# A float32 matmul of 256 tokens issued as two of 128, in the first product of a feed-forward

## The chip, the core and the metric

The kernel runs on one NeuronCore of a Trainium2 chip. The metric is the device time of one execution in microseconds; smaller is better. The engines are named as the profile names them: PE (TensorE matmuls), PEld (TensorE weight loads), DVE (VectorE), ACT (ScalarE), POOL (GpSimd) and SP (SyncE, which issues most transfers).

## What is computed

Attention in which a query sees only the keys of its own hash bucket, for 4 x 8 heads of 768 tokens and 64 features; its output, as 3072 tokens of 512 features, goes through a feed-forward with 2048 hidden features and a gate. Everything is float32.

```python
def _attn_ref(q, k, v, proj):
    ...
    mask = q_bucket[:, :, :, None] == k_bucket[:, :, None, :]
    scores = scale * np.matmul(q, k.transpose(0, 1, 3, 2))
    scores = np.where(mask, scores, -1000000000.0)
    ...
    return np.matmul(attn, v).astype(np.float32)

def _moe_ref(x, w_in, w_out):
    h = x @ w_in
    sp = np.maximum(h, 0.0) + np.log1p(np.exp(-np.abs(h)))
    g = h * erf(sp)
    return (g @ w_out).astype(np.float32)
```

The change lies in `h = x @ w_in`, called the first product here; `g @ w_out` is the second.

## The kernel before

Attention comes first, for 16 pairs of heads, and takes until about 312 us of the profiled execution. Its matmuls stand at L387 and L856 (hash bits), L568 (scores `st`, a bfloat16 part and a float32 part, two heads in the two row halves of the array), L653 (`av`, two heads in the two column halves), and L697 (the sums of the softmax). Ten small matmuls at L817 (`warm`) stand ahead of it. The feed-forward follows. An `If` on a flag that the kernel computes chooses between finishing this feed-forward and a slower general way with a feed-forward of its own; the profiled execution runs one feed-forward.

The feed-forward works on 6 tiles of 512 tokens. Each tile has 4 blocks of hidden features, so there are 24 blocks `p`. Both products use Strassen's scheme in Winograd's form: operands are cut into quarters, and 7 products of quarters take the place of 8; for one block a product is [2 x 128 hidden features] x [256 features] x [256 tokens].

The function `product(p, name, where, first, last)` issues one of the seven, P1 to P7. Its result fills a PSUM tile of 128 partitions x 2 x 256 float32 (one bank): partition and `u` are the hidden feature, the last axis is the token. The loop over `u` takes the two halves of the hidden features, that over `kc` the two halves of the 256 features that are summed over. So a product is 4 matmul instructions (L1257), each with 128 x 128 weights `a[:, kc, f : f + P]` (a slice of `w_in_sb` or of sums in `area`) and 256 moving columns `b[:, kc, :]`, the tokens. `start` on the very first clears the bank's accumulation, the later ones add. In the first three blocks (`FILL`) the results go to the banks M1 to M7 and X, later always to the bank X.

After a product either `read` (L1275, ACT copies the bank to `h`) or `complete` (L1279, DVE adds the bank to `h`) empties it. The gate follows on ACT (L1287, L1291, L1308) and DVE (L1297, L1312). `project` (L1375) issues the second product, one instruction at a time, 28 per block, into the banks M1 to M7, which collect over the 4 blocks of a tile.

The order of the work is not written by hand: `arrange` simulates the engines with fixed costs (1.73 for a `product`, 0.432 for a `project`), ranks and dependences, and the operations are emitted in the order it finds. On PE a product alternates with about four instructions of `project` once the pipeline is filled. The program marks its last matmul for the engine that waits for the bank, and its first matmul waits until the bank was emptied.

Of the kernel before, what the change touches and what calls it, by code (L numbers as in the profile page):

```python
# [63 lines left out]
P = 128  # L64
# [133 lines left out]
def kernel(  # L198
# [11 lines left out]
    nc = tc.nc  # L210
# [47 lines left out]
    for ab in range(2):  # L258
        rows = slice(ab * D, ab * D + D)
        nc.vector.tensor_copy(  # L260
            out=proj_sb[rows, ab * QR : ab * QR + NBIT],
# [5 lines left out]
    for c, (end, factor) in enumerate(  # L267
# [12 lines left out]
            out=steps[:, c : c + 1],  # L280
# [9 lines left out]
    for ab in range(2):  # L290
        rows = slice(ab * D, ab * D + D)
        nc.vector.tensor_copy(
            out=proj_q[rows, ab * QB : ab * QB + NBIT],
# [12 lines left out]
    def bank(name):  # L306
        if "X" in kept:
            return kept["X"]
        return misc.tile([P, 512], F32, name=name, tag="bank")
# [907 lines left out]
    def feed_forward(pools, check, late):  # L1217
        again = late is None
        work, outp, sums, hp = (pools[name] for name in ("work", "outp", "sums", "hp"))
        if True:  # L1220
# [8 lines left out]
            def product(p, name, where, first, last):  # L1229

                t, c = divmod(p, NC4)
                d = st[p]
                x = blocks[t % 2]
                b11, t3 = x[:, 0:2, 0:TH], x[:, 0:2, TH:T]
                b21, b22 = x[:, 2:4, 0:TH], x[:, 2:4, TH:T]
                t1, t2, t4 = (x_sum[:, n, :, :] for n in range(3))
                a11, a12 = w_in_sb[:, 0:2, 0:FH], w_in_sb[:, 2:4, 0:FH]
                s3, a22 = w_in_sb[:, 0:2, FH:DFF], w_in_sb[:, 2:4, FH:DFF]
                s1, s2, s4 = (w_sum[:, n, :, :] for n in range(3))
                a, b = dict(  # L1240
                    P1=(a11, b11),
                    P2=(a12, b21),
                    P3=(s4, b22),
                    P4=(a22, t4),
                    P5=(s1, t1),
                    P6=(s2, t2),
                    P7=(s3, t3),
                )[name]
                if first:
                    if where == "X":  # L1250
                        d[where] = bank("X")[:, :].rearrange("p (u t) -> p u t", u=2)
                    else:
                        d[where] = kept[where]
                for u in range(2):
                    f = (2 * c + u) * P
                    for kc in range(2):
                        nc.tensor.matmul(  # L1257
                            out=d[where][:, u, :],
                            lhsT=a[:, kc, f : f + P],
                            rhs=b[:, kc, :],  # L1260
                            start=(first and u == 0 and kc == 0),
                            stop=(last and u == 1 and kc == 1),
                            skip_group_check=True,
                        )

            def quarter(p, q):

# [184 lines left out]
            def first_ops(p):  # L1452
# [25 lines left out]
                for k, (name, where, q, fn) in enumerate(steps):  # L1478
# [5 lines left out]
                    if chain["P"]:  # L1484
# [4 lines left out]
                        1.73,  # L1489
                        (0, p, k),  # L1490
                        product,
                        (p, name, where, name in ("P1", "P2", "P5"), name in ("P4", "P2", "P3")),
                        after=after,
# [217 lines left out]
            for t in range(1, NTILE):  # L1711
                first, last = (t - 1) * NC4, t * NC4 - 1
# [165 lines left out]
```

## Time and profile before

| | us |
|---|---|
| median of 2 runs | 900.13 (900.12 to 900.14) |
| span of the profiled execution | 898.4 |
| attention, until the first matmul of L1257 | 312.5 |
| from the first to the last matmul of L1257 | 312.5 to 854 |
| last matmul of the second product starts | about 894 |

The profiled execution's own time isn't listed apart from its span; the runs' median lies 1.7 us above the span.

In the profile's views a row is a group of instructions: line, engine, operation, tile written <- tiles read, shape, and xcount. In the line's view two numbers follow, busy microseconds and the mean nanoseconds of one; in the timeline a row begins with the start and the length of the group in microseconds from the span's start. A shape of `128*128 128x256` for PE is rows*columns of the array that are used, then the partitions x columns that stream through. PE and PEld are the two halves of TensorE and can be busy at the same time. Matmuls are pipelined: the recorded duration of one is longer than the distance between two.

### The profile page before, as it was taken

The numbers are of one execution on the slowest core, as the hardware profiler recorded it, in microseconds if no ns is written. First come the engines' busy times: TensorE is split into PE (matmuls) and PEld (weight loads), VectorE is DVE, ScalarE is ACT, GpSimd is POOL, SyncE is SP. The second block draws the span as 40 slices with busy tenths as digits, with TensorE's granted clock in tenths as the row PEclk, the third lists the DMA queues.
The fourth block names the chain that finished last, engine by engine and source line by source line (L and its number), as shares of the span: only waits on it lengthen the run. The fifth ranks groups of instructions, "written<-read, shape, count | busy, mean of one in ns | idle before, by whom it ended". The sixth has DMA issues, their size and how long they took to land.

```text
span 898.4 us, 12500 instructions
## 1 busy us (share of the span) xinstructions
PE 893.6 (99%) x4888; PEld 664.0 (74%) x4888; DVE 667.1 (74%) x836; ACT 577.4 (64%) x808; POOL 58.1 (6%) x97
## 2 busy tenths in 40 slices
PE   9999999999999999999999999999999999999998
PEld 5544444444444588888888888888888888888887
DVE  5999999999999879996566556656776556655653
ACT  6888888788887668855555455555655555545520
POOL 1111211111110000000000001000100000000000
PEclk9999999999999999999999999999999999999999
DMA  9557655676651322201231014211321123101321
GB/s 231 132 159 192 188 163 142 182 192 193 165 146 61 102 89 65 82 35 71 59 95 58 25 47 106 82 36 47 99 89 36 36 59 94 35 11 47 97 72 49
DMA packets 65203, 86.95 MB, mean 97 GB/s; under 512 B 34430, under 2 KB 47790, under 8 KB 65136
## 3 DMA queue, kind: packets, MB, share of 16 engines
q1 hardware_dynamic: 56192, 63.55, 25.0%
q0 software_dynamic: 8224, 21.80, 8.6%
q8 instruction: 40, 0.66, 0.3%
q10 hardware_dynamic: 720, 0.72, 0.2%
q14 instruction: 27, 0.22, 0.1%
HBM read 64.71 MB, written 17.40 MB: 91 GB/s over the span
## 4 chain that ended last, share of the span: by engine, by line
PE 99%; DVE 0%; ACT 0%; issue 0%; DVEq 0%
PE M L1375 32%; PE X L1257 29%; PE st L568 17%; PE av L653 14%; PE M L1257 4%; PE bits L856 1%; PE bits L697 1%; PE warm L817 0%; PE X L1375 0%; PE bits L387 0%; PE z_ps L697 0%; DVE u L1412 0%; PE X L697 0%; ACT e_even L595 0%; DVE w L1412 0%; ACT both L400 0%
## 5 line engine op out<-in xcount | busy, mean ns | idle before, releaser
L1297 DVE SCALAR_TENSOR_TENSOR e<-w,e 128x1024 f32<-128x1024 f32 x144 | 173.6, 1220 | 8.4 <-ACT w L1291 3.3
L1257 PE MATMUL X<-area,w_in_sb 128*128 128x256 f32 x680 | 160.6, 379 | 0.0
L1291 ACT ACTIVATE w<-h,cq 128x1024 f32<-128x1024 f32 x144 | 155.5, 1136 | 0.0
L568 PE MATMUL st<-q,k 64*128 64x384 f32 x768 | 155.2, 483 | 0.0
L1279 DVE TENSOR_TENSOR h<-X,h 128x512 f32<-128x512 f32 x65 | 44.7, 688 | 144.8 <-PE X L1257 144.8
L1257 PEld LDWEIGHTS X<-area,w_in_sb 128*128 128x128 f32 x680 | 129.2, 190 | 17.6
L1375 PE MATMUL M<-w_out_sb,h 128*128 128x256 f32 x576 | 141.5, 379 | 0.0
L1257 PE MATMUL X<-area 128*128 128x256 f32 x520 | 122.8, 379 | 0.0
L1275 ACT COPY h<-X 128x512 f32<-128x512 f32 x85 | 49.3, 580 | 112.8 <-PE X L1257 112.6
L1375 PEld LDWEIGHTS M<-w_out_sb,h 128*128 128x128 f32 x576 | 109.4, 190 | 14.9
L1257 PEld LDWEIGHTS X<-area 128*128 128x128 f32 x520 | 98.8, 190 | 13.4
L1287 ACT ACTIVATE e<-h,cq 128x1024 f32<-128x1024 f32 x48 | 55.0, 1148 | 79.3 <-DVE h L1279 79.1
L1375 PE MATMUL M<-wt,S 128*128 128x256 f32 x384 | 95.4, 379 | 0.1
L568 PEld LDWEIGHTS st<-q,k 64*128 64x128 f32 x768 | 69.2, 187 | 35.1 <-issue 33.7
L641 DVE TENSOR_TENSOR area<-area 128x1536 f32<-128x1536 f32 (+1 forms) x46 | 79.2, 1721 | 6.7 <-ACT area L595 5.4
L1375 PEld LDWEIGHTS M<-wt,S 128*128 128x128 f32 x384 | 72.9, 190 | 10.4 <-issue 0.5
L595 ACT ACTIVATE e_even<-st 128x768 f32<-128x768 f32 x96 | 73.9, 818 | 0.5 <-PE st L568 0.5
L595 ACT ACTIVATE area<-st 128x768 f32<-128x768 f32 x90 | 72.7, 810 | 0.3 <-PE st L568 0.3
L653 PE MATMUL av<-e_even,v 128*64 128x385 f32 x384 | 65.7, 490 | 0.0
L568 PE MATMUL st<-both 64*128 64x384 bf16 x384 | 63.9, 324 | 0.2 <-ACT e_even L595 0.2
L1312 DVE TENSOR_TENSOR h<-h,e 128x1024 f32<-128x1024 f32 x48 | 58.0, 1220 | 4.0 <-ACT e L1308 4.0
L653 PE MATMUL av<-area,v 128*64 128x384 f32 x360 | 60.6, 486 | 0.0
(135 smaller groups left out, 965.5 us busy)
## 6 DMA issues: line engine op xcount, KB each, us to landing
wt<-wt SPq DMA_DIRECT2D x24, 768.0 KB, 4.3
raw<-in_w_out_dram POOLq DMA_DIRECT2D x16, 512.0 KB, 4.1
raw<-in_w_in_dram POOLq DMA_DIRECT2D x14, 512.0 KB, 4.4
v<-in_v_dram SPq DMA_DIRECT2D x32, 192.0 KB, 4.8
q<-in_qkT_dram SPq DMA_DIRECT2D x30, 192.0 KB, 3.9
k<-in_qkT_dram SPq DMA_DIRECT2D x30, 192.0 KB, 4.6
r<-rd SPq DMA_DIRECT2D x30, 192.0 KB, 3.8
xs<-x SPq DMA_DIRECT2D x15, 384.0 KB, 3.1
```

Of the source, the lines that this page charges most:

```text
L568: nc.tensor.matmul(out=st[:, ab, 0:HS], lhsT=d["k" + src][rows, keys], rhs=d["q" + src][rows, cols], start=(part == 0), stop=(part == 1),)
L595: nc.scalar.activation(out=e[:, :, 0:HS], in_=st[:, :, 0:HS], func=AF.Exp, scale=scale)
L641: nc.vector.tensor_tensor(out=into, in0=one, in1=two, op=ALU.add)
L653: nc.tensor.matmul(out=d["av", half][rows, 0:w], lhsT=d["v"][:, g * GC + c, rows], rhs=e[:, ab, 0:w], start=(g == 0 and c == 0), stop=(g = ...
L1257: nc.tensor.matmul(out=d[where][:, u, :], lhsT=a[:, kc, f : f + P], rhs=b[:, kc, :], start=(first and u == 0 and kc == 0), stop=(last and ...
L1275: nc.scalar.copy(out=quarter(p, q), in_=st[p][where])
L1279: nc.vector.tensor_tensor(out=h, in0=st[p][where], in1=h, op=ALU.add)
L1287: nc.scalar.activation(out=s, in_=unit(p, v), func=AF.Sigmoid, bias=cq[:, n : n + 1])
L1291: nc.scalar.activation(out=q, in_=unit(p, v), func=AF.Sigmoid, scale=GATE_S[j][0], bias=cq[:, j : j + 1])
L1297: nc.vector.scalar_tensor_tensor(out=s, in0=st[p].pop(("q", v, j)), scalar=GATE_S[j][2], in1=s, op0=ALU.add, op1=ALU.mult,)
L1312: nc.vector.tensor_tensor(out=h, in0=h, in1=st[p].pop(("s", v)), op=ALU.mult)
L1375: nc.tensor.matmul(out=banks["last" if apart and sub else name][:, sub, :], lhsT=a[:, u, sub * P : (sub + 1) * P], rhs=b[:, u, :], start=( ...
```

## The change

Inside `product`, each of the four matmul instructions becomes two, one after the other, with the same weights: the first for tokens 0 to 127 of the quarter, the second for tokens 128 to 255. Each output element gets the same terms in the same order. `start` is now on the first of the eight, `stop` on the last of the eight. Nothing else is edited; the planner's costs are the same.

```diff
                 for u in range(2):
                     f = (2 * c + u) * P
                     for kc in range(2):
-                        nc.tensor.matmul(
-                            out=d[where][:, u, :],
-                            lhsT=a[:, kc, f : f + P],
-                            rhs=b[:, kc, :],
-                            start=(first and u == 0 and kc == 0),
-                            stop=(last and u == 1 and kc == 1),
-                            skip_group_check=True,
-                        )
+                        for th in range(2):
+                            tokens = slice(th * P, th * P + P)
+                            nc.tensor.matmul(
+                                out=d[where][:, u, tokens],
+                                lhsT=a[:, kc, f : f + P],
+                                rhs=b[:, kc, tokens],
+                                start=(first and u == 0 and kc == 0 and th == 0),
+                                stop=(last and u == 1 and kc == 1 and th == 1),
+                                skip_group_check=True,
+                            )
```

The order of PE's program at the start of the feed-forward, where the last `av` of attention gives way to the first products; a row names the line, the operation, the tile written (M_3066 to M_3068 are the banks M1, M2 and M4) and its sources, the columns and the count. This is the difference of the two programs:

```order
 L653 MATMUL av<-v 64x384 x2
-L1257 MATMUL M_3066<-area,w_in_sb 128x256 x4
-L1257 MATMUL M_3067<-area,w_in_sb 128x256 x4
-L1257 MATMUL M_3066<-area 128x256 x4
-L1257 MATMUL M_3068<-area 128x256 x4
+L1259 MATMUL M_3066<-area,w_in_sb 128x128 x8
+L1259 MATMUL M_3067<-area,w_in_sb 128x128 x8
+L1259 MATMUL M_3066<-area 128x128 x8
+L1259 MATMUL M_3068<-area 128x128 x8
 L697 MATMUL X<-area,ones 32x384 x4
```

Four instructions of 256 columns became eight of 128 in the same place, with two lines more above them.

PE's program before, where the first `project` (L1375) enters between products, after 80 instructions of L1257:

```order
L1257 MATMUL X<-area 128x256 x4
L1375 MATMUL M_3066<-w_out_sb,h 128x256
L1257 MATMUL M_3072<-area,w_in_sb 128x256 x4
L1257 MATMUL X<-area,w_in_sb 128x256 x4
L1375 MATMUL M_3066<-w_out_sb,h 128x256 x3
```

And the same place of the changed program:

```order
L1259 MATMUL X<-area 128x128 x8
L1377 MATMUL M_3066<-w_out_sb,h 128x256
L1259 MATMUL M_3072<-area,w_in_sb 128x128 x8
L1259 MATMUL X<-area,w_in_sb 128x128 x8
L1377 MATMUL M_3066<-w_out_sb,h 128x256 x3
```

Nothing moved past anything else. In the branch that the profiled execution runs, the rows of DVE, ACT, POOL and SP are the same as before but for the line numbers, and the waits stand where they stood.

## The prediction

> **What bounds the kernel now.** I read the page first: the span, each engine's busy time, and the chain of work that ended last.
>
> ```profile
> span 898.4 us, 12500 instructions
> ...
> PE 893.6 (99%) x4888; PEld 664.0 (74%) x4888; DVE 667.1 (74%) x836; ACT 577.4 (64%) x808; POOL 58.1 (6%) x97
> ...
> PE 99%; DVE 0%; ACT 0%; issue 0%; DVEq 0%
> PE M L1375 32%; PE X L1257 29%; PE st L568 17%; PE av L653 14%; PE M L1257 4%; PE bits L856 1%; PE bits L697 1%; PE warm L817 0%; PE X L1375 0%; PE bits L387 0%; PE z_ps L697 0%; DVE u L1412 0%; PE X L697 0%; ACT e_even L595 0%; DVE w L1412 0%; ACT both L400 0%
> ```
>
> TensorE's matmuls are 99% of the chain. The changed line, L1257, is 29% + 4% of it, the second product (L1375) 32%, attention the rest. A busy PE need not be PE at its best, so I looked at who waits. In the view of waits ScalarE and VectorE wait for the first product; PE itself is listed with 1.2 us in all:
>
> ```profile
> DVE h L1279 <- PE X L1257: 144.8, 42, 8.1
> ACT h L1275 <- PE X L1257: 112.6, 61, 3.3
> ...
> PE warm L817 <- DVE ones L254: 1.0, 1, 1.0
> PE st L568 <- ACT e_even L595: 0.2, 1, 0.2
> ```
>
> So every nanosecond that a matmul of L1257 gains or loses moves the end by as much, until some other engine stops it; a slower PE meets nobody, since the others already wait for it.
>
> Next, the pace. A stretch of the timeline where one product follows another (columns: start, length, engine, line, tiles, shape, count):
>
> ```profile
> 408.01 1.70 PEld L1257 LDWEIGHTS X<-area,w_in_sb 128*128 128x128 f32 x8
> ...
> 408.23 1.89 PE L1257 MATMUL X<-area,w_in_sb 128*128 128x256 f32 x8
> ```
>
> A product call issues 4 float32 instructions and the trace has 8 loads and 8 matmuls: each instruction is two passes, each with a load of its own (PEld) and a matmul. From the line's view, with the durations min/median/max in ns:
>
> ```profile
> L1257 PE MATMUL X<-area,w_in_sb x680: 379/379/379, 340.0 to 847.9; 128*128 128x256 f32 x170
> ...
> L1257 PE MATMUL X<-area x520: 379/379/380, 343.5 to 853.9; 128*128 128x256 f32 x174
> L1257 PEld LDWEIGHTS M<-area,w_in_sb x88: 186/190/190, 312.5 to 350.4; 128*128 128x128 f32 x88
> L1257 PE MATMUL M<-area,w_in_sb x88: 379/379/483, 312.5 to 350.6; 128*128 128x256 f32 x88
> ...
> L1257 PE MATMUL M<-area x56: 379/379/379, 316.0 to 343.3; 128*128 128x256 f32 x56
> ```
>
> One matmul is recorded as 379 ns, yet 8 take 1.89 us: they start (1.89 - 0.379) / 7 = 0.2159 us apart. That distance, 215.9 ns per pass of 256 columns, is what a pass costs; 379 contains a tail that lies under the next pass. There are 680 + 520 + 88 + 56 = 1344 passes, which is 24 blocks x 7 products x 4 instructions x 2, so 1344 x 215.9 ns = 290.2 us of the span, the 33% of the chain.
>
> **The change, part by part.** It removes 1344 passes of 256 columns and adds 2688 of 128, each with a load of 128 columns of weights, as before. Order and waits of all engines in the executed program stay as they are. Three things are to be priced.
>
> 1. The stream of a 128-column pass. The trace has float32 passes of 384 columns, two at a time in the two column halves of the array, so 24 records are 12 starts, 11 steps:
>
> ```profile
> 98.04 4.04 PE L653 MATMUL av<-area,v 128*64 128x384 f32 x24
> ...
> L653 PE MATMUL av<-area,v 128*64 128x384 f32 x360 | 60.6, 486 | 0.0
> ```
>
> (4.04 - 0.49) / 11 = 322.7 ns a step, 0.49 being the duration of one (486 ns in the line's view). So 128 columns more cost 322.7 - 215.9 = 106.8 ns, and a pass of no columns would cost 215.9 - 2 x 106.8 = 2.3 ns. A 128-column pass then takes 215.9 - 106.8 = 109.1 ns, if streaming sets it. The rows have hundredths of a microsecond, so each distance is good to about 0.7 ns and the 2.3 to about 2.
>
> 2. The load. Its record is 190 ns long, longer than the new pass, so the question is how much of that the next matmul has to wait for. Today 215.9 ns of streaming hide it. Where it is not hidden it can be measured; PE starts here on empty weights, right after another mode of the array:
>
> ```profile
> 332.86 1.59 PEld L1257 LDWEIGHTS M<-area,w_in_sb 128*128 128x128 f32 x8
> 332.86 1.99 PE L1257 MATMUL M<-area,w_in_sb 128*128 128x256 f32 x8
> ```
>
> Against 1.89 for eight matmuls in the steady stretch these take 1.99: the first waits 0.10 us for its weights (its record is the 483 of the line's view, 104 ns over 379). And 8 loads take 1.59 against 1.70: six of the seven steps at 215.9 leave 1.59 - 0.19 - 6 x 0.2159 = 0.105 us between the first load and the second. So a load holds the path for about 105 ns, not 190, and the next can begin as soon as its matmul streams. In the new rhythm load and stream run side by side, 105 ns against 109.1: the stream still sets the pace, by a hair. I take 109.1.
>
> From below: if the 2.3 ns were not paid per pass at all, two passes would cost 2 x 106.8 = 213.6, 2.3 ns less than today. From above: the one load that ran with no stream beside it is recorded with 186 ns, those under a stream with 190 (line's view above). If these 4 ns belong to the load itself and come on top of the 109.1, a pass is 113.1.
>
> 3. Instruction supply. PE gets 2 instructions (load and matmul) per 109.1 ns in a product, 54.6 ns each, where it got one per 108. The densest 10 us of attention and its whole stretch show what has been supplied so far:
>
> ```profile
> 44.50:54.50 10.00, 10.00 (x82) 5.66 (x82) 9.49 (x14) 8.86 (x14) 3.30 (x6) 1.00 0.75 204
> 20.00:280.00 260.00, 260.00 (x1848) 127.18 (x1846) 245.51 (x323) 223.09 (x391) 40.35 (x72) 1.00 0.61 165
> ```
>
> 164 instructions in 10 us are one per 61 ns, 3694 in 260 us one per 70. For most of the feed-forward a product (32 instructions then, 1.75 us) alternates with a projection (16, 1.73 us): 48 in 3.48 us, one per 72 ns, which attention kept up for 260 us. Only the fill is denser: the program's order has 80 of the 672 instructions of L1257 before the first of L1375, 640 loads and matmuls. At 61 instead of 54.6 ns they would cost 4.1 us more. I take 0, hidden by what is queued, and keep 4 for the range. Code is fetched by a queue that is busy 0.3% of the time; the 2688 added instructions don't load it:
>
> ```profile
> q8 instruction: 40, 0.66, 0.3%
> ```
>
> Sum: 1344 x (2 x 109.1 - 215.9) ns = 1344 x 2.3 ns = +3.1 us. Nothing hides it and nothing is late behind it. The span becomes 898.4 + 3.1 = 901.5. The median of the two runs, 900.13, is 1.7 us above this span, so the time is 903.2. By the bounds: -3.1 us (897.0) without any cost per pass, 1344 x (226.2 - 215.9) = +13.8 us (913.9) with 4 ns more per load, 918 with the fill's 4.1 as well.
>
> A rule that speaks against this: the Trainium skill, "TensorE: Matmul & The Clock Gate", section "Back-to-back issue gap", says that in a real stream of load and matmul pairs a matmul of 128 columns comes every ~81 ns, against 56 ns for matmuls alone: 25 ns more per pass that neither load nor stream explains. By it, as an estimate, a pass here would be 109.1 + 25 = 134.1 ns and the sum 1344 x (268.2 - 215.9) = +70 us, so 970. No row here has both at once, a load as long as the stream; the two rows of step 2 speak for 109.
>
> **The rivals.**
>
> *Load and stream don't overlap fully (slower).* The 105 ns of step 2 were read with nothing streaming. Under a stream, the tightest case is in the scores, where float32 weights load while a bfloat16 pair streams; first the loads, then the matmuls:
>
> ```profile
> 10.51 0.36 PEld L568 LDWEIGHTS st<-q,k 64*128 64x128 f32 x4
> ...
> 10.51 0.34 PE L568 MATMUL st<-both 64*128 64x384 bf16 x2
> 10.67 0.82 PE L568 MATMUL st<-q,k 64*128 64x384 f32 x4
> ```
>
> The loads begin at 10.51, the matmuls that need them at 10.67: at most 0.16 us under a stream, and there the stream of 384 columns needed that long anyway. So the price of a pass is anywhere between 113 and 161 ns: 914 up to 1344 x (322 - 215.9) = +142.6 us, 1043; the middle, 137 ns, gives +78 us and 978. The point from which it decides: 2% of 900 is 18 us, 13.4 ns per old pass, so a new pass of more than 114.7 ns. That is only 5.6 ns above my value, so it is a serious rival. The skill's 81 ns lie on this side.
>
> *A 128-column pass has a floor (slower).* The only passes of this width in the profile look terrible:
>
> ```profile
> 0.99 4.26 PE L817 MATMUL warm<-ones 128*64 128x128 f32 x19 [0.99 <-DVE ones L254]
> ...
> 332.65 0.28 PE L1775 MATMUL X<-stats,ones 64*1 64x64 f32 x4
> ...
> L817 PE MATMUL warm<-ones 128*64 128x128 f32 x20 | 4.4, 414 | 1.0 <-DVE ones L254 1.0
> ...
> L1775 PE MATMUL X<-stats,ones 64*1 64x64 f32 x4 | 0.3, 214 | 0.0
> ...
> L817 PEld LDWEIGHTS warm<-ones 128*64 128x64 f32 x20 | 4.1, 228 | 1.0 <-DVE ones L254 1.0
> ```
>
> The warm-up's matmuls start (4.26 - 0.41) / 18 = 214 ns apart (the means of the line's view, 414 and 214 ns, are the durations). As a floor per pass that would be 1344 x (428 - 215.9) ns = +285 us: 1185. Against it: they are the first thing PE does, and the four 64-column passes at 332.65, 0.21 us long each, all start within 0.07 us. The Trainium skill, "TensorE: Matmul & The Clock Gate", section "What's actually happening", gives half the clock for about the first 3.4 us of work, and the trace agrees: 214 is twice the 106.8 of step 1. The page's granted clock shows nothing of it.
>
> *Instruction supply (within 2%).* Step 3 at its upper bound: 907.
>
> *The change doesn't do what it says:* that the second half skips its load since the weights are the same. The 10 warm-up instructions share their weights too, and the profile has 20 loads for them; in any case the stream would still be the bound, and the time as forecast.
>
> **How the numbers follow.** A measurement of this kernel tells about 2% from no change. My case, stream and load side by side at 109 to 113 ns: 0.73, all of it within 2%. Instruction supply: 0.03, also within. Load and stream not fully overlapped: 0.21, slower. The floor or something else that costs as much: 0.02, slower. Faster by over 2% would need 18 us out of 290 that already run at streaming pace: 0.01. So faster 0.01, same 0.76, slower 0.23. The time is that of my case, 903.2. Its own range with the supply is 897 to 918, holding 0.76; to reach 0.8 I go on into the second case, whose 0.21 spread evenly over 914 to 1043 gives 0.04 for the 22 us up to 940. Range 897 to 940.
>
> **What would show it.** The changed line should have 2688 loads and 2688 matmuls. Sixteen matmuls in a row should start 109 ns apart; 113 means the 4 ns are in the load, over 115 means the first rival, and then PEld's starts should follow the matmuls late, or the matmuls should begin well after the loads. PE should still be 99% busy, with L1375's passes at 215.9 and attention unchanged up to 312 us. If the products of the fill, 312 to 350 us, run slower than later ones, it is instruction supply. What would make me wrong most likely is that a load beside a stream of equal length is not free.

## The result, and the profile after

The changed kernel takes 910.9 us (910.87 to 910.94, 2 runs) against 900.13. The ratio is 1.0117 with an interval of 1.0088 to 1.0146, and 1.0114 [1.0097, 1.0131] in the repeat below, so it is slower by 1.1%, clear of the measurement's own spread and within the 2% that I had called no change. Forecast were 903.2 us and a range of 897 to 940.

From the page of the changed kernel, the same lines as before:

```profile
span 909.1 us, 15188 instructions
...
PE 904.1 (99%) x6232; PEld 710.1 (78%) x6232; DVE 667.9 (73%) x836; ACT 577.1 (63%) x808; POOL 58.1 (6%) x97
...
PE 99%; DVE 0%; ACT 0%; issue 0%; DVEq 0%
```

PE has 1344 loads and 1344 matmuls more, and it still is 99% busy and 99% of the chain: nobody new ends last. The page's 40 slices show what did change. These are the rows of the weight loads, first before the change, then after it:

```profile
PEld 5544444444444588888888888888888888888887
```

```profile
PEld 5545444444444699999999999999999999999987
```

The loads were busy for eight tenths of the feed-forward and are now at nine tenths or more. Inside a product they are never idle. That alone does not say that the loads set the pace: a load is recorded as about 190 ns, longer than the distance of two new passes, so the row would be full with passes 109 ns apart as well. The timeline of the changed kernel, where one product follows the second product's matmuls:

```profile
400.63 1.97 PEld L1259 LDWEIGHTS X<-area,w_in_sb 128*128 128x128 f32 x16
400.85 1.95 PE L1259 MATMUL X<-area,w_in_sb 128*128 128x128 f32 x16
```

And the same place in the view by windows (the stretch and its length, busy us of PE, PEld, DVE, ACT, POOL, then the granted clock, the DMA share and GB/s):

```profile
401.00:402.40 1.40, 1.40 (x15) 1.40 (x14) 1.37 (x4) 1.40 (x3) 0.00 (x0) 1.00 0.04 12
```

Sixteen matmuls start (1.95 - 0.275) / 15 = 111.7 ns apart, not 109.1; 0.275 is the duration of one in the line's view of the changed kernel:

```profile
L1259 PEld LDWEIGHTS X<-area,w_in_sb x1360: 189/192/193, 341.3 to 858.3; 128*128 128x128 f32 x195
L1259 PE MATMUL X<-area,w_in_sb x1360: 272/275/276, 341.4 to 858.4; 128*128 128x128 f32 x195
```

The single records of the trace give the same with more digits. This table is worked out from them: distances of consecutive starts inside one line's runs, those of 300 ns and more left out (4 and 2 before, 0 and 2 after).

```
kernel    line             columns   distances   mean ns
before    first product    256       1190        215.9
before    second product   256       1194        215.8
after     first product    128       2538        111.7
after     second product   256       1194        216.1
```

A pass of the first product went from 215.9 to 2 x 111.7 = 223.4, so 1344 x 7.5 ns = 10.1 us. That accounts for the difference: from the first matmul of the feed-forward to the start of its last the records take 581.9 us before and 592.1 after, +10.1. The remaining 0.6 of the span's 10.7 lies ahead of the change: the first scores start at 5.94 us before and 6.51 after, where the code is the same.

### The profile page after: what moved, and what is told of

Same layout as the page of the kernel before. It is cut to its first block, busy times and chain, and to the rows that moved or that the text cites. A ratio compares the mean times of both kernels' runs of the same rounds, so it can differ in the third digit from the quotient of the medians.

```text
span 909.1 us, 15188 instructions
## 1 busy us (share of the span) xinstructions
PE 904.1 (99%) x6232; PEld 710.1 (78%) x6232; DVE 667.9 (73%) x836; ACT 577.1 (63%) x808; POOL 58.1 (6%) x97
## 4 chain that ended last, share of the span: by engine, by line
PE 99%; DVE 0%; ACT 0%; issue 0%; DVEq 0%
PE M L1377 32%; PE X L1259 29%; PE st L568 17%; PE av L653 14%; PE M L1259 4%; PE bits L856 1%; PE bits L697 1%; PE warm L817 0%; PE X L1377 0%; PE bits L387 0%; PE z_ps L697 0%; DVE u L1414 0%; PE X L697 0%; ACT e_even L595 0%; DVE w L1414 0%; ACT both L400 0%
## 5 line engine op out<-in xcount | busy, mean ns | idle before, releaser
L1259 PEld LDWEIGHTS X<-area,w_in_sb 128*128 128x128 f32 x1360 | 165.1, 192 | 4.2
L1259 PE MATMUL X<-area,w_in_sb 128*128 128x128 f32 x1360 | 165.6, 275 | 0.0
L1259 PEld LDWEIGHTS X<-area 128*128 128x128 f32 x1040 | 126.2, 192 | 3.2
L1259 PE MATMUL X<-area 128*128 128x128 f32 x1040 | 126.6, 275 | 0.0
L1377 PEld LDWEIGHTS M<-w_out_sb,h 128*128 128x128 f32 x576 | 104.7, 191 | 11.4
L1377 PEld LDWEIGHTS M<-wt,S 128*128 128x128 f32 x384 | 68.6, 191 | 7.5 <-issue 0.7
```

The source lines that it names most:

```text
L1259: nc.tensor.matmul(out=d[where][:, u, tokens], lhsT=a[:, kc, f : f + P], rhs=b[:, kc, tokens], start=(first and u == 0 and kc == 0 and th ...
L1377: nc.tensor.matmul(out=banks["last" if apart and sub else name][:, sub, :], lhsT=a[:, u, sub * P : (sub + 1) * P], rhs=b[:, u, :], start=( ...
```

## Experiments

My theory after the result: **the load sets the pace.** A matmul cannot start before its weights are in, the next load cannot start before that matmul has, and this loop takes 111.7 ns for 128 columns, a little more than the 109.1 in which 128 columns stream. Rivals: **the stream's side** (a narrow pass pays 5 ns instead of about 2.5, whatever is loaded), and **instruction supply** (one per 55.8 ns and no faster).

**The changed kernel again**, without an edit.

> The changed kernel once more, to know its time and its pace well. All theories: 910.9 us; 2688 passes of the first product 111.7 ns apart. The 0.6 us by which attention ended later in the changed profile is chance of the first microseconds, so the first pass of the first product may start anywhere from 312.4 to 313.2 us.

Measured: 910.63 us (910.5 to 911.38, 4 runs) against 900.26 (899.88 to 900.78, 7 runs), ratio 1.0114 [1.0097, 1.0131]; 111.7 ns per pass and 592.1 us of feed-forward as in the first profile. The first product starts at 313.57 us here, outside the 312.4 to 313.2 that I had allowed. It isn't the first microseconds that are late: the first scores start at 5.76 us, earlier than in the first profiles of before (5.94) and of the change (6.51). The time is lost inside attention, most of it in one wait of PE for a transfer, at 27 us, which the view of waits of the first changed profile doesn't have:

```profile
PE st L568 <- DMA both<-bd: 1.0, 1, 1.0
```

So the start of the feed-forward moves for more than one reason (312.48, 313.06 and 313.57 us in these three profiles), and the spans of the seven runs of before range from 898.1 to 899.0.

**192 + 64 tokens.** The same number of instructions, cut unevenly.

```diff
-                        for th in range(2):
-                            tokens = slice(th * P, th * P + P)
+                        cuts = (0, 192, 256)
+                        for th in range(len(cuts) - 1):
+                            tokens = slice(cuts[th], cuts[th + 1])
...
-                                stop=(last and u == 1 and kc == 1 and th == 1),
+                                stop=(last and u == 1 and kc == 1 and th == len(cuts) - 2),
```

> The same number of passes as the changed kernel, but cut 192 + 64 tokens instead of 128 + 128. Theory 'the load sets the pace' (a pass shorter than its successor's load waits for that load, 111.7 ns): 162.5 ns after a pass of 192, 111.7 after one of 64, 274.2 for the pair against 215.9, 1344 x 58.3 = +78 us, 978 us. Rival 'a narrow pass pays about 5 ns instead of 2.5 on the stream's side' or rival 'instructions come no faster than one per 55.8 ns': the pair stays at 223.3, 910 to 911 us.

Measured: 978.5 us (one run). With as many passes, instructions and streamed columns as the changed kernel it takes 68 us more. The stream's side can't give that. Instruction supply can't either if instructions are queued while a wide pass streams; if nothing is queued, a pass of 64 would wait for its two instructions (2 x 55.8 = 111.6 ns) just as for a load, and this cut doesn't tell the two apart. The shorter loads below do. Here the line's view shows the wait inside the records, where the minimum and the maximum of a matmul's duration are two shapes:

```profile
L1260 PEld LDWEIGHTS X<-area,w_in_sb x1360: 190/190/192, 346.9 to 925.4; 128*128 128x128 f32 x195
L1260 PE MATMUL X<-area,w_in_sb x1360: 219/300/382, 347.0 to 925.4; 128*128 128x64 f32 x98, 128*128 128x192 f32 x97
```

The records of eleven consecutive starts (ns after 501000) show how: `L` is a load, `M` a matmul with its columns and duration.

```
L 222  M 276 (64, 275)  L 332  M 388 (192, 382)  L 444  M 606 (192, 326)
L 608  M 769 (64, 219)  L 771  M 825 (64, 275)   L 881
```

A matmul is recorded as started when the stream before it is through; if its weights aren't there it stands and waits, and its record is longer by that: 275 and 382 where its like without a wait has 219 and 326, 56 ns each. The loads start 110, 112, 164 and 163 ns apart: after a pass of 64 the load's loop decides, after one of 192 the stream. I had expected the 111.7 to show between the starts of the matmuls (162.5, 162.5, 111.7, 111.7); by these records it shows between the loads, and the starts of the matmuls read 162.5, 55.8, 111.7 and 218. The sum of four is the same 548.

**160 + 96 tokens**, priced from the rule before it ran; the edit is as above with `cuts = (0, 160, 256)`.

> Cut 160 + 96 tokens: a price worked out beforehand from the rule, pass = the larger of 111.7 ns (load) and 2.5 + columns x 0.8333 ns (stream). The pass of 160 takes 135.8, that of 96 takes 111.7 where the stream needs 82.5: 247.5 a pair, 1344 x (247.5 - 215.9) = +42.5 us, 943 us. The rivals that pay per pass on the stream's side or per instruction give 910 us, as for 128 + 128.

Measured: 942.8 us (one run).

**Four times 64 tokens**, `cuts = (0, 64, 128, 192, 256)`.

> Each instruction of the first product cut into four of 64 tokens: 5376 loads of 128 columns. 'The load sets the pace': 111.7 ns each although the stream needs 53, 1344 x (446.8 - 215.9) = +310 us, 1210 us; if a load is quicker with less stream beside it, its pace is 105 to 109 ns and the time 1180 to 1200. 'The stream's side pays 5 ns per pass': 4 x 58.4 = 233.6, +24 us, 924 us. 'Instruction supply' gives 1210 as well, so this run prices the load and rules out the stream only.

Measured: 1210.1 us (one run). The timeline of a product:

```profile
497.58 3.76 PEld L1260 LDWEIGHTS X<-area,w_in_sb 128*128 128x128 f32 x32
...
497.80 3.68 PE L1260 MATMUL X<-area,w_in_sb 128*128 128x64 f32 x32
```

The first load starts under a wide pass, 0.216 us ahead of the second; the other 30 steps take (3.76 - 0.192 - 0.216) / 30 = 111.7 ns. A load's loop is as long with 53 ns of stream beside it as with 107: it isn't slowed by the stream.

**Shorter loads at unchanged streams.** Half of the instructions load 96 columns instead of 128.

```diff
+                        m = P if kc == 0 else 96
                         for th in range(2):
                             tokens = slice(th * P, th * P + P)
                             nc.tensor.matmul(
-                                out=d[where][:, u, tokens],
-                                lhsT=a[:, kc, f : f + P],
+                                out=d[where][0:m, u, tokens],
+                                lhsT=a[:, kc, f : f + m],
```

> As the changed kernel, but the second half of the sum over features (kc = 1) goes to 96 of the 128 hidden features of each group, so half of the loads have 96 columns; a quarter of the hidden features gets half of its sum. Streams, passes, instructions and PSUM columns stay as they are. 'The load sets the pace': the distance to a matmul that follows a 96-column load falls to the stream's 109.2, the others stay at 111.7; 1344 x 2.5 = -3.4 us against the changed kernel, 907.5 us. 'The stream's side' and 'instruction supply': 111.7 everywhere, 910.9 us.

Measured: 907.27 us (906.94 to 907.68, 4 runs), ratio to before 1.0077 [1.006, 1.0094]. It is 3.4 us less than the 910.63 of the repeat, as priced for the load. In the line's view (busy, mean ns of one):

```profile
L1260 PEld LDWEIGHTS X<-area,w_in_sb 128*128 128x128 f32 x680 | 95.8, 191 | 4.3
L1260 PEld LDWEIGHTS X<-area,w_in_sb 128*96 128x96 f32 x680 | 83.7, 164 | 0.0
```

32 columns less are 27 ns less per load. The matmuls behind the two kinds of load differ by the wait in their record:

```profile
L1260 PE MATMUL X<-area,w_in_sb 128*128 128x128 f32 x680 | 103.5, 275 | 0.0
L1260 PE MATMUL X<-area,w_in_sb 128*96 128x128 f32 x680 | 102.0, 273 | 0.0
```

In the single records of one product the matmuls start at (ns after 502000, the four marked * after a load of 96 columns):

```
211   322*   431*   541*   650*   759   871   982
```

From the second short load until the first long one after them the steps are 109, 110, 109 and 109 ns, elsewhere 111 or 112. Averaged over the 146 products that stand alone between matmuls of the second product, these four steps are 109.1 to 109.2 ns, and those behind long loads 111.6 to 111.7. So with the load out of the way a narrow pass costs what the stream was priced at, and the stream's side and instruction supply fall, queued or not: neither the streamed columns nor the number of instructions changed.

The edit also narrows the results to 96 partitions. That isn't what counts. The start of a stream is the recorded start plus the 2.4 ns by which a waiting record is longer (275.0 against 272.6 on average). By these starts the last pass with 128 columns of weights takes 109.2 ns when a short load follows, and the last with 96 takes 111.6 when a long one follows: the pace goes with the next load, not with the width of the pass's own result.

**Other neighbours.** `th` outside of `kc`, so that no two instructions in a row have the same weights:

```diff
-                    for kc in range(2):
-                        for th in range(2):
+                    for th in range(2):
+                        for kc in range(2):
```

> The changed kernel with the loops over th and kc exchanged, so that two instructions in a row no longer have the same weights; the same number of passes and columns. 'The load sets the pace': each pass loads anew whatever was loaded before, so 111.7 ns and 910.7 us as the changed kernel, within 0.1%. If repeated weights cost or save something in the load (the same SBUF columns read twice, or a load cut short), the time moves by more than 2 us.

Measured: 910.55 us (910.01 to 910.75, 4 runs), ratio 1.0114 [1.0097, 1.013], 111.7 ns per pass. That the weights are the same as those just loaded neither saves nor costs anything.

**The second product cut instead of the first**, in `project`, from the kernel before:

```diff
+                for half in range(2):
+                    cols = slice(half * P, half * P + P)
...
-                    out=banks["last" if apart and sub else name][:, sub, :],
+                        out=banks["last" if apart and sub else name][:, sub, cols],
...
-                    rhs=b[:, u, :],
+                        rhs=b[:, u, cols],
...
```

`start` stays with the first half of the first instruction, `stop` with the second half of the last.

> The first product as before the change; instead each instruction of the second product (1344 passes too, other weights, other banks, sums kept over 28 instructions) is issued as two of 128 columns. 'The load sets the pace' holds for any 128-column load: 111.7 ns per pass, up to 1344 x (223.4 - 215.9) = +10.1 us, somewhat less because the first narrow pass after a wide one takes 109.2: 909 to 910.5 us. If the price came from the first product alone (its operands, its bank X that is emptied each time), the passes would be at 109.1 and the time 903.5 us.

Measured: 911.76 us (911.73 to 912.21, 4 runs), ratio 1.013 [1.0113, 1.0147], 111.6 ns per pass. The price per pass is not the first product's own. The time is 1.3 us above the upper end that I gave. Most of it is one wait close to the end, where the last matmuls follow the kernel's branch (a COMPARE_BRANCH on PE's sequencer ends just before them in both traces); before the change and with this cut:

```profile
891.07 0.19 PEld L1375 LDWEIGHTS M<-wt,S 128*128 128x128 f32 x1 [0.48 <-issue]
```

```profile
902.55 1.86 PEld L1377 LDWEIGHTS M<-wt,S 128*128 128x128 f32 x16 [1.44 <-issue]
```

`issue` is a wait for which the profile shows no cause. It is 1.0 us longer, and no run here tells why; that it is the fetch of code behind the branch would be a guess.

## Why the prediction came out as it did

No change at 2%, and a time inside the range, was right, and 910.9 lies inside 897 to 918, the part of the range that stood for my own case. But the 903.2 came from the wrong winner in step 2. That this cost only 7.7 us is luck of this cut, in which the stream and the load's loop lie 2.5 ns apart.

**What bounds the kernel, and that nothing would hide the cost:** right. PE is 99% of the chain before and after, and 7.5 ns on each of 1344 passes come out as 10.1 us at the end.

**Step 1, the stream, 109.1 ns:** right. Behind the shorter loads the passes start 109.2 ns apart. The straight line through the passes of 256 and 384 columns was enough for it.

**Step 2, the load:** this step failed. "A load holds the path for about 105 ns, not 190" was right in kind; the record's length is no price. But "the stream still sets the pace, by a hair" was wrong: the load sets it, with 111.7 ns. The 105 came from rows in hundredths of a microsecond, as a small difference of large numbers; I had claimed an error of 0.7 ns for distances found from several equal steps, and then used this single one without any. The single records of that place in the kernel before (ns from the span's start, duration in brackets) say more:

```
332858 load   332860 matmul (483)   332967 load   333180 matmul
```

The second load starts 109 ns after the first, already at my stream's pace, and in a steady chain of loads each turn takes 2 to 3 ns more. So rounding is the larger part of the error, and the rest is that I took a single load for the price of a chain. The 104 ns beside it were read to the nanosecond, but they tell when the first matmul can go on (332860 + 104 = 332964), not when the next load begins. So the term 2.3 ns per old pass was mis-sized: it measured 7.5, and +3.1 us became +10.1. Where I compared two durations that differ by a few per cent, I owed the reader both possible winners as a forecast, not only as a bound. The prediction's last sentence feared that "a load beside a stream of equal length is not free"; the place was right, but it isn't the stream beside it: the fourfold cut has the same 111.7 with half the stream.

**The bound from above, 113.1 ns:** it held, 111.7 is inside, but for another reason. I had added 4 ns because loads under a stream are recorded with 190 instead of 186. By the fourfold cut the stream beside it doesn't stretch the load's loop.

**Step 3, instruction supply at 0:** right. With 96-column loads the same number of instructions comes faster, and with 192 + 64 it comes slower. In the changed kernel the passes of the fill are as fast as later ones; leaving out the three gaps above 200 ns and one of 142, those before 352 us are 111.7 ns apart, those after it 111.5.

**The first rival** put a price of 113 to 161 ns on overlap that isn't full. It stood on the right side, above the stream, but its range begins above 111.7 and the overlap is full; the longer of two parallel loops counts, not their sum. The Trainium skill, "TensorE: Matmul & The Clock Gate", section "Back-to-back issue gap", puts the difference between 56 and 81 ns down to the load, which the formula for matmuls alone leaves out. The prediction read it as 25 ns that neither load nor stream explains and added it to 109.1, which gave its estimate of 134 ns and 970 us. The trace has 111.7 and 910.9: the load does count in the spacing, but for these float32 passes the measurement decides against the added 25 ns.

**The floor** fell: a stream of 64 columns is through after 56 ns (from 769 to 825 in the records of 192 + 64). **That a second load of the same weights is skipped** fell too: 2688 loads are recorded, and the order of the loops makes no difference (910.55 us).

Still open: why a load's turn is 2 to 3 ns longer in a chain than alone. In the products of the changed kernel the third load starts 110.1 ns after the second on average, the later ones 111.5 to 111.8 apart; no run here separates the parts of that turn. (The first distance of the matmuls, 109.2, is the stream's: the first pass has its load done under the second product, and the second is recorded as started when the first stream is through.)

## What to carry to other kernels

Price a float32 matmul pass here as the longer of two parallel loops: 2.5 ns + 0.833 ns per streamed column (measured from 64 to 384 columns), and 111.7 ns for loading 128 columns of weights. Up to about 131 streamed columns ((111.7 - 2.5) / 0.833) the load decides, and every further cut adds a whole load's 111.7 ns; the rule gave 943, 978 and 1210 us beforehand for three other cuts, and 942.8, 978.5 and 1210.1 were measured. A load's loop is read from where loads follow one another without a wide stream between them, not from the length of its record (190), and if that place yields a single step, its rounding belongs into the range.

## What I had not expected of the hardware

A matmul without its weights is recorded as running: the wait stands inside its duration (219 becomes 275 for 64 columns, 326 becomes 382 for 192, 272.6 becomes 275.0 for 128), so PE looks 99% busy and idle for 0.0 us while it waits for loads. Nor does a load row without gaps tell: the loads of 96 columns have 0.0 us of idle time before them too, though there the stream sets the pace, because a record of 164 ns covers a distance of 109. What tells is the matmul's own duration beside that of its like with the load out of the way.
